# A LayerNorm's transposes moved from TensorE to a DMA in 16-bit halves, with rings of their own

## The chip, the core and the metric

The kernel runs on one core of one Trainium2 chip. The metric is device time in microseconds (us) of one launch, the median of several runs. A core has TensorE (PE in the profile, its weight loads PEld), VectorE (DVE), ScalarE (ACT), GpSimd (POOL) and SyncE (SP), which here issues the DMA transfers. Each engine takes its instructions in a fixed order and waits on semaphores for data, and for a buffer to come free.

## The reference

One transformer block over 2048 rows of 512, with modulation from a condition vector `c`:

```python
mod = (_silu(c) @ w_mod).reshape(c.shape[0], 6, 1, -1)
sa, ca, ga, sb, cb, gb = (mod[:, 0], ..., mod[:, 5])
h = _layernorm(x) * (1 + ca) + sa
x = x + ga * attention(h, k_cache, v_cache, wq, wo)   # 32 heads of 128, 8 kv heads, last 512 keys
h = _layernorm(x) * (1 + cb) + sb
x = x + gb * ((_gelu(h @ w_gate) * (h @ w_up)) @ w_down)   # inner width 1792
```

All inputs and the output are fp32. The text below is about the second LayerNorm, for the first 1024 of the 2048 rows, and about the tiles that hold the products of the feed-forward part.

## The kernel before

**Numbers.** Every matmul operand is an fp16 pair: a high half (the value rounded) and a low half (the rest), so a product is three matmuls (`mm3`, L86). To make a pair, ACT copies the fp32 tile to the high half and POOL or DVE subtracts it for the low half (`halves`, L154; `split_post`, L738; `parts`, L1295).

**Rows and stages.** The rows come in 16 tiles of 128, a query block is four tiles, a half of the attention is two query blocks. Attention runs as 128 units (half, pair of heads, query block, head) of four steps each; a step is one 128x512 score tile. For step t PE makes the scores `ps` (two PSUM banks in turn), DVE their maximum `nm` (L982), ACT the exponential `ee` (L991), ACT and DVE the two halves of the probabilities (`high` L1001, `low` L1006), and SP transposes both halves by one DMA, `pt<-p` (L1012). Two units later PE multiplies by the values (`po`, `pv_tasks` L926); its first product of a unit needs all four transposes of that unit. `pv_post` (L772) turns `po` into an `ot` pair: ACT writes the high half, DVE the low half a step later. When the four heads of a set have their `ot`, PE multiplies them with the output weights (`py`, `y_tasks` L940), one row tile per unit, 12 matmuls a tile, and DVE adds the result to the tile's `acc` (L952).

**Order of the work.** In the attention part every engine follows the program's order (`manual_schedule`, L1536). Work is put into named places: `at(("w", step), fn)` runs at the end of a step, `sched` (L608) puts a load some steps before its first use. The main loop (L1539 to L1584) goes through a step as scores, maximum, low half and transpose of an older tile, exponential, high half of an older tile, three queued PE groups, then loads, then "w" places. In the feed-forward part SP keeps the program's order, and a planner orders the other engines by simulated times.

**Rings.** `pool.tile(..., tag, bufs)` takes a slot of the ring `tag`, any free one; if none is free, the first instruction that writes the new tile waits until all readers of an older tile are done. Those that matter here:

- `ot`, 12 slots of 2 KB a partition (`NOT`, L43): the attention's `ot` pairs; `sbc` (L130), written at the start and read by `mod_col` (L135, L137) up to step 286; four early tiles; and in the feed-forward part all `at` pairs.
- `raw`, 5 slots: loads that are used once; the `stage` tiles of the weight preparation (`staged`, L1341); and the `hf` tile of the second LayerNorm (L504).
- `acc` in PSUM, 5 banks: most PE results, and the transposed LayerNorm tile `pln` (L498).
- `rw`, 2 slots: raw weights; `h`, 14 blocks of transposed activations; `gs`, one slot.

**The second LayerNorm, first 1024 rows.** When a tile of the first half has its last `py`, `attn_final` (L958) stores it and starts `ln_tile(2, ...)` (L476) on the `acc` tile in place. `now` is the step at which that happens; the eight tiles have it some three to five steps apart, from step 258 on. The steps are put at `now` plus 1, 5, 8, 9, 10, 12, 13 (L965): `stat` (DVE statistics, POOL power), `norm` (POOL, L239), `turn` (PE: four fp32 transposes of 128x128 into one `pln` bank, L500), `affine` twice (ACT, two 128x128 pieces each, PSUM to the fp32 tile `hf`, L508; the second also stores `hf` to DRAM as `hs`), `parts` twice (ACT high halves L520, POOL low halves L522, into the blocks). At `now` plus 12 the next rows are loaded into the `acc` ring. The blocks are used in the feed-forward part, from about step 480 on.

**Weights for the feed-forward part.** From step 286 on `prep_set` (L1349) loads gate and up weights into `rw`, measures them (`f_spread`, L297: POOL after PE and DVE), and POOL scales them, splits them into `stage` tiles and makes their combinations (L1356); SP stores each `stage` tile and loads the next weights when the `rw` slots are free. The first set has its POOL work at steps 290 to 296, the next set's loads come at steps 296 and 297.

**Feed-forward part.** For each pair n of column blocks the gated product has four parts. For ten of the fourteen passes (`turned(n)`, L293) the output product is made from three of them and four differences: `sums_of` (L1300) makes, on POOL, the differences t1, t3, t2, t4 and their pairs (`parts`), which PE reads in `yt_tasks` (L1696).

Of the kernel before, what the change touches and what calls it, by code (L numbers as in the profile page):

```python
# [10 lines left out]
F32 = mybir.dt.float32  # L11
# [28 lines left out]
GU = 2.0 ** -38  # L40
PRE = 2.0 ** -20
TINY = 1e-36
NOT = 12  # L43
LDGAP = 1
NRAW = 5
NRW = 2
# [18 lines left out]
def block_kernel(ctx: ExitStack, tc: tile.TileContext, x, kT, v, wq, wo, wg, wu, wd, cT, wc, wm, out):  # L65
# [410 lines left out]
    def ln_tile(gen, i, src):  # L476
        jsc, jsh = ln_cols("a" if gen < 2 else "f")
        qb, i = divmod(i % (2 * QT), QT)
        st = {}

        def load():
            if gen == 2:
                st["x"] = src()
            else:
                st["x"] = raw("xs")
                dma(st["x"], src())

        def stat():
            ln_stat(st["x"], st)
            ln_power(st)  # L490

        def norm():
            if gen == 2:
                return pool_ts(st["x"], st["x"], st["mv"][:, 0:1], st["rs"], ALU.subtract, ALU.mult)
            nc.vector.tensor_scalar(st["x"], st["x"], st["mv"][:, 0:1], st["rs"], op0=ALU.subtract, op1=ALU.mult)

        def turn():
            st["ps"] = bank("acc", "pln", NACC)  # L498
            for dt in range(KT):
                nc.tensor.transpose(st["ps"][:, dt * P:(dt + 1) * P], st["x"][:, dt * P:(dt + 1) * P], ident)  # L500

        def affine(dts):
            if 0 in dts:
                st["f"] = raw("hf") if gen == 2 else tmp("hf")  # L504
            f = st["f"]
            for dt in dts:
                sl = slice(dt * P, (dt + 1) * P)
                nc.scalar.activation(f[:, sl], st["ps"][:, sl], AF.Identity,  # L508
                                     scale=cols[:, jsc, dt:dt + 1], bias=cols[:, jsh, dt:dt + 1])
            if KT - 1 in dts:  # L510
                dma(spilled(gen, qb)[:, :, i * P:(i + 1) * P], f.rearrange("p (k q) -> p k q", k=KT))

        def parts(act):
            o = slice(i * P, (i + 1) * P)
            f = st["f"].rearrange("p (k q) -> p k q", k=KT)
            for h, name in enumerate(("b11", "b21") if qb == 0 else (None, "b22")):
                if name:
                    t, src = block(gen, name), f[:, 2 * h:2 * h + 2, :]
                    if act:
                        nc.scalar.activation(t[:, 0:2, o], src, AF.Copy)  # L520
                    else:
                        nc.gpsimd.tensor_tensor(t[:, 2:4, o], src, t[:, 0:2, o], op=ALU.subtract)  # L522

        more = [lambda: parts(True), lambda: parts(False)]
        return load, [stat, norm, turn, lambda: affine((0, 1)), lambda: affine((2, 3))] + more

    TURN = {}

# [429 lines left out]
    def attn_final(ti):  # L958
        y1[ti] = dram.tile([P, D], F32, name=f"y{ti}")
        dma(y1[ti], acc[ti])  # L960
        if ti < 2 * QT:
            nxt = ti + 2 * QT
            own, steps = ln_tile(2, ti, lambda: acc[ti])
            own()
            for d, fn in zip((1, 5, 8, 9, 10, 12, 13), steps):  # L965
                at(("w", now[0] + d), fn)
            at(now[0] + 12, lambda: load_acc(nxt, rows_of(x, nxt)))
        else:
            ln_last(ti - 2 * QT)
# [294 lines left out]
    def f_items(q, hold=None):  # L1264
# [28 lines left out]
                    sums_of()  # L1293

        def parts(key, g, eng):  # L1295
            t = A[n, key] = pair("ot", "at", NOT)
            nc.scalar.activation(t[:, 0, :], g, AF.Copy)  # L1297
            eng.tensor_tensor(t[:, 1, :], g, t[:, 0, :], op=ALU.subtract)

# [484 lines left out]
```

## Time and profile before

| What | Time |
|---|---|
| median of three runs | 1743.84 us |
| lowest and highest of them | 1743.32 and 1745.21 us |
| the profiled execution | 1743.57 us |
| its span, first to last instruction | 1741.8 us |
| PE busy in the span | 1714.7 us |
| first and last transpose of the eight tiles | 700.4 and 775.5 us |

Times within the trace count from the start of the span. In a row of groups stand line, engine, operation, output tile, input tiles, shapes and count, then busy time, mean duration in ns, and the idle time of the engine just before with what ended it. In a row about one tile the three numbers are shortest, median and longest duration in ns, then first and last start in us. A row of a timeline has start, duration, engine, line and tiles; in brackets the idle time before it and what ended that. PE's matmuls overlap by about 0.16 us, so what a PE group costs is read from start to start.

### The profile page before, as it was taken

To read this page: it belongs to the slowest core of one execution; us is meant where nothing else is said; L and a number is where in the kernel's file an instruction comes from. 1 tells how busy PE (TensorE), PEld (TensorE's weight loads), DVE (VectorE), ACT (ScalarE), POOL (GpSimd) and SP (SyncE) were. 2 spreads that over 40 slices of the span, in tenths; PEclk is the share of its full clock that TensorE was granted. 3 is DMA by queue.
4 is the path that set the end of the run, shared out by engine and by line. 5 is a ranking of instruction groups with operands and counts; after the bars stand their busy time and mean duration, and the time that the engine had idled before them with its cause. 6 is when DMAs were issued, how large, how long until landed. Compare 5 with 4: busy or idle time off the path is not lost.

```text
span 1741.8 us, 26188 instructions
## 1 busy us (share of the span) xinstructions
PE 1714.7 (98%) x8022; PEld 787.0 (45%) x8022; DVE 1417.6 (81%) x2454; ACT 1258.5 (72%) x2813; POOL 1045.9 (60%) x1266
## 2 busy tenths in 40 slices
PE   7999999999999999999999999999999999999998
PEld 5444444444444444444444444444444444444443
DVE  7898898888888899888888788888886678556674
ACT  6988788888878777898778778787784554643344
POOL 4889778776788884654675665754621558313422
PEclk9999999999999999999999999999999999999999
DMA  7999999999999999999999999899986663743235
GB/s 236 218 205 211 213 214 207 223 206 221 215 217 228 205 205 187 212 213 230 201 219 224 208 223 220 186 235 218 197 180 150 187 177 128 191 139 100 91 97 167
DMA packets 690636, 339.82 MB, mean 195 GB/s; under 512 B 578880, under 2 KB 601408, under 8 KB 690496
## 3 DMA queue, kind: packets, MB, share of 16 engines
q1 hardware_dynamic: 690208, 337.63, 85.5%
q8 instruction: 63, 1.03, 0.3%
q14 instruction: 77, 0.63, 0.1%
q10 hardware_dynamic: 288, 0.52, 0.1%
HBM read 135.66 MB, written 61.87 MB: 113 GB/s over the span
## 4 chain that ended last, share of the span: by engine, by line
PE 82%; ACT 5%; DVE 5%; DMA 3%; POOL 2%; issue 2%; SPq 0%; ACTq 0%; DVEq 0%; POOLq 0%
PE py L90 19%; PE ps L90 17%; PE po L90 17%; PE qa L90 8%; PE fa L90 6%; PE qc L90 4%; PE fc L90 3%; PE ya L90 2%; PE qb L90 2%; PE fb L90 2%; PE yc L90 1%; ACT ee L991 1%; DMA yv<-yu 1%; ACT p L1003 1%; DVE nm L982 1%
## 5 line engine op out<-in xcount | busy, mean ns | idle before, releaser
L991 ACT ACTIVATE ee<-ps,nm 128x512 f32<-128x512 f32 x512 | 350.1, 684 | 191.9 <-DVE nm L982 189.3
L1008 DVE SCALAR_TENSOR_TENSOR p<-ee,rr,p 128x512 f16<-128x512 f32 x512 | 460.0, 898 | 4.5 <-ACT p L1003 3.9
L982 DVE TENSOR_REDUCE nm<-ps 128x1 f32<-128x512 f32 x512 | 350.4, 684 | 106.1 <-PE ps L90 103.2
L90 PE MATMUL ps<-k,qt 128*128 128x512 f16 x1536 | 414.9, 379 | 5.6 <-ACT ee L991 4.4
L1003 ACT ACTIVATE p<-ee,rr 128x512 f16<-128x512 f32 x512 | 364.6, 712 | 19.0 <-DVE rr L999 10.0
L90 PE MATMUL po<-pt,v 128*128 128x512 f16 x1536 | 373.0, 379 | 2.7 <-DVE kmax L183 1.4
L90 PE MATMUL py<-wo,ot 128*128 128x512 f16 x1536 | 371.5, 379 | 0.1
L90 PEld LDWEIGHTS <-w 128*128 128x128 f16 x2184 | 213.3, 98 | 263.3 <-issue 4.7
L90 PEld LDWEIGHTS <-v 128*128 128x128 f16 x1536 | 149.9, 98 | 184.9 <-DMA pt<-p 2.3
L90 PEld LDWEIGHTS <-ot 128*128 128x128 f16 x1536 | 150.3, 98 | 181.7 <-DVE ot L740 0.5
L90 PEld LDWEIGHTS <-qt 128*128 128x128 f16 x1536 | 145.9, 98 | 176.9 <-issue 4.7
L1303 POOL TENSOR_TENSOR fg<-fg 128x512 f32<-128x512 f32 x40 | 51.8, 1295 | 135.6 <-DVE fg L1287 103.0
L740 DVE SCALAR_TENSOR_TENSOR ot<-po,ot 128x512 f16<-128x512 f32 x128 | 87.7, 685 | 39.1 <-ACT ot L739 38.6
L1297 ACT ACTIVATE at<-fg 128x512 f16<-128x512 f32 x86 | 53.4, 625 | 64.8 <-DVE fg L1287 44.5
L991 ACT ACTIVATION_READ_ACCUMULATOR ee<-ps,nm 128x1 f32 x512 | 99.9, 195 | 0.0
L952 DVE SCALAR_TENSOR_TENSOR acc<-py,ysc,acc 128x512 f32<-128x512 f32 x128 | 94.7, 740 | 6.2 <-PE py L90 6.2
L235 POOL TENSOR_TENSOR lw<-lw,half__86 128x1 f32<-128x1 f32 x37 | 23.4, 633 | 104.2 <-DVE lw L185 104.1
L90 PE MATMUL fa<-t,w 128*128 128x512 f16 x336 | 83.6, 379 | 1.9 <-ACT u L885 1.4
L90 PE MATMUL qa<-t,w 128*128 128x512 f16 x348 | 84.9, 379 | 0.0
L397 POOL TENSOR_TENSOR rs<-rs,nhalf 128x1 f32<-128x1 f32 x32 | 18.8, 586 | 103.6 <-DVE rs L391 100.7
L739 ACT ACTIVATE ot<-po 128x512 f16<-128x512 f32 x128 | 73.8, 577 | 5.0 <-PE po L90 5.0
L1657 DVE SCALAR_TENSOR_TENSOR yt<-ya,dyc,yt 128x512 f32<-128x512 f32 x68 | 50.1, 745 | 22.1 <-PE ya L90 21.7
(241 smaller groups left out, 2794.0 us busy)
## 6 DMA issues: line engine op xcount, KB each, us to landing
w<-kept SPq DMA_DIRECT2D x123, 256.0 KB, 3.3
wo<-kept SPq DMA_DIRECT2D x70, 256.0 KB, 3.4
kept<-stage SPq DMA_DIRECT2D x61, 256.0 KB, 3.3
raw<-in_wo SPq DMA_DIRECT2D x56, 256.0 KB, 3.2
kept<-w SPq DMA_DIRECT2D x39, 256.0 KB, 3.4
rw<-in_wq SPq DMA_DIRECT2D x38, 256.0 KB, 3.2
hs<-hf SPq DMA_DIRECT2D x32, 256.0 KB, 2.9
pt<-p SPq DMA_TRANSPOSE x512, 3.5
```

The costliest lines, as they stand in the source:

```text
L90: nc.tensor.matmul(ps, a, b, start=first and n == 0, stop=last and n == 2, skip_group_check=chain)
L235: nc.gpsimd.tensor_tensor(out, out, half_, op=ALU.pow)
L739: nc.scalar.activation(t[:, 0, :], src, AF.Copy, scale=scale)
L740: return lambda: nc.vector.scalar_tensor_tensor(t[:, 1, :], src, scale, t[:, 0, :], op0=ALU.mult, op1=ALU.subtract)
L952: nc.vector.scalar_tensor_tensor(acc[ti], st["p"], by, acc[ti], op0=ALU.mult, op1=ALU.add)
L982: nc.vector.tensor_reduce(nm, E[t]["ps"], axis=AX.X, op=ALU.max, negate=True)
L991: nc.scalar.activation(e, E[t]["ps"], AF.Exp, bias=E[t]["nm"], scale=1.0, accum_out=sm[:, t % 2:t % 2 + 1])
L1003: nc.scalar.activation(p16[:, 0, :], E[t]["e"], AF.Copy, scale=E[t]["r"])
L1008: nc.vector.scalar_tensor_tensor(p16[:, 1, :], E[t]["e"], E[t]["r"], p16[:, 0, :], op0=ALU.mult, op1=ALU.subtract)
L1297: nc.scalar.activation(t[:, 0, :], g, AF.Copy)
L1303: nc.gpsimd.tensor_tensor(g[o], g[a], g[b], op=ALU.subtract)
L1657: nc.vector.scalar_tensor_tensor(YT[key], ps, by, YT[key], op0=ALU.mult, op1=ALU.add)
```

## The change

The change touches three places.

1. `ln_tile` for the second LayerNorm's first rows (gen 2) no longer transposes on PE. ACT writes the high fp16 half of the normalised tile, POOL the low half, both into one pair of a new ring `lnh` of four slots. SP transposes the pair by one DMA, as for the probabilities, into a tile with a single slot: for even tiles a new tag `lnt`, for odd tiles the ring `gs`. POOL adds the two transposed halves into an fp32 tile `hf`, which also lies in `lnh`. ACT's affine then reads and writes that tile in place. `raw` holds no `hf` any more, and PSUM no `pln` of these tiles.
2. The steps are put at `now` plus 1, 5, 8, 9, 12, 16, 19, 20, 22, 23: statistics and `norm` as before, high half, low half, DMA transpose, sum, the two affines, the two block halves.
3. The ring `ot` has 10 slots instead of 12. In the feed-forward part the pairs of t1, t2 and t3 lie in `lnh`, that of t4 in `lnt`; the other `at` pairs stay in `ot`.

```diff
-NOT = 12
+NOT = 10
...
+        def high():
+            st["h"] = pair("lnh", "lnh", 4)
+            nc.scalar.activation(st["h"][:, 0, :], st["x"], AF.Copy)
+
+        def low():
+            nc.gpsimd.tensor_tensor(st["h"][:, 1, :], st["x"], st["h"][:, 0, :], op=ALU.subtract)
+
+        def turn_dma():
+            st["t"] = pool.tile([P, 2, KT, P], F16, tag="gs" if i % 2 else "lnt", name="lnt", bufs=1)
+            nc.sync.dma_start_transpose(st["t"].rearrange("p h k q -> p (h k) q"), st["h"].rearrange("p a b -> p (a b)"))
+
+        def joined():
+            st["f"] = pool.tile([P, D], F32, tag="lnh", name="hf", bufs=4)
+            nc.gpsimd.tensor_tensor(st["f"].rearrange("p (k q) -> p k q", k=KT), st["t"][:, 0], st["t"][:, 1], op=ALU.add)
+            st["ps"] = st["f"]
+
         def affine(dts):
-            if 0 in dts:
-                st["f"] = raw("hf") if gen == 2 else tmp("hf")
+            if 0 in dts and gen < 2:
+                st["f"] = tmp("hf")
...
-        return load, [stat, norm, turn, lambda: affine((0, 1)), lambda: affine((2, 3))] + more
+        turns = [high, low, turn_dma, joined] if gen == 2 else [turn]
+        return load, [stat, norm] + turns + [lambda: affine((0, 1)), lambda: affine((2, 3))] + more
...
-            for d, fn in zip((1, 5, 8, 9, 10, 12, 13), steps):
+            for d, fn in zip((1, 5, 8, 9, 12, 16, 19, 20, 22, 23), steps):
...
-            t = A[n, key] = pair("ot", "at", NOT)
+            t = A[n, key] = pair(*{"t4": ("lnt", "at", 1)}.get(key, ("lnh", "at", 4) if key[0] == "t" else ("ot", "at", NOT)))
```

## The prediction

> **What bounds the kernel now.** I read the profile page first, then the groups by engine, then busy time by stretch, then the timelines of PE, POOL, ACT and SP around the places that the diff touches.
>
> ```profile
> PE 1714.7 (98%) x8022; PEld 787.0 (45%) x8022; DVE 1417.6 (81%) x2454; ACT 1258.5 (72%) x2813; POOL 1045.9 (60%) x1266
> ...
> PE 82%; ACT 5%; DVE 5%; DMA 3%; POOL 2%; issue 2%; SPq 0%; ACTq 0%; DVEq 0%; POOLq 0%
> ```
>
> PE is the bound: 98% busy, and 82% of the chain. So a PE instruction that goes is time that goes, unless PE then waits for an engine that it used to be behind. The change lies where PE has little to give away but the others are loaded too:
>
> ```profile
> 700.00:800.00 100.00, 99.04 (x478) 47.01 (x477) 86.55 (x162) 85.78 (x212) 53.57 (x58) 1.00 0.99 213
> ```
>
> The columns are PE, PEld, DVE, ACT and POOL busy, the granted clock, and the DMA share, 0.99.
>
> **The change part by part.** *Out: the PE transposes.* Eight tiles with four transposes each are the 32 of this row:
>
> ```profile
> L508 ACT ACTIVATE hf<-pln,cols x64: 440/452/483, 239.3 to 782.0; 128x128 f32<-128x128 f32 x64
> ...
> L500 PE MATMUL pln<-ident,acc x32: 272/273/300, 700.4 to 775.5; 128*128 128x128 f32 x32
> ```
>
> Durations overlap on PE, so I price a tile by starts.
>
> ```profile
> 700.39 0.60 PE L500 MATMUL pln<-ident,acc 128*128 128x128 f32 x4
> 700.83 0.81 PE L90 MATMUL ps<-k,qt 128*128 128x512 f16 x3
> ...
> 730.84 0.81 PE L90 MATMUL po<-pt,v 128*128 128x512 f16 x3
> 732.28 0.63 PE L500 MATMUL pln<-ident,acc 128*128 128x128 f32 x4 [0.63 <-POOL w L158]
> ...
> 774.02 0.81 PE L90 MATMUL po<-pt,v 128*128 128x512 f16 x3
> 775.15 0.63 PE L500 MATMUL pln<-ident,acc 128*128 128x128 f32 x4 [0.33 <-ACT hf L508]
> ```
>
> From 700.39 to 700.83 a tile takes 0.44 us; eight are 3.5 us. A group of three matmuls takes about 0.65 us by starts (184.83 to 185.50, further down, is one), so the tile at 732.28 came 0.79 us late (1.44 less 0.65) and the one at 775.15 0.48 us late. Both waited for something only the transposes need (I read it as the PSUM bank that ACT still drains), so 1.27 us goes too. **Gross gain 4.8 us.**
>
> *In: split, DMA transpose, sum.* The nearest rows do the same operations elsewhere:
>
> ```profile
> L543 ACT ACTIVATE xh<-xs x8: 612/616/631, 1362.8 to 1399.3; 128x512 f16<-128x512 f32 x8
> L544 POOL TENSOR_TENSOR xh<-xs,xh x8: 1152/1161/1559, 1363.5 to 1401.3; 128x512 f16<-128x512 f32 x8
> L549 SPq DMA_TRANSPOSE xt<-xh x8: 1231/1240/1479, 1364.6 to 1410.4; - x8
> L522 POOL TENSOR_TENSOR b<-hf,b x24: 665/672/1124, 245.7 to 790.5; 128x256 f16<-128x256 f32 x24
> L1303 POOL TENSOR_TENSOR fg<-fg 128x512 f32<-128x512 f32 x40 | 51.8, 1295 | 135.6 <-DVE fg L1287 103.0
> ```
>
> Per tile: ACT 0.62 us, POOL 1.16 us for the low half, SP 1.24 us of issue. The sum of two f16 tiles into f32 is not in the trace: between 1.16 us (L544) and 1.30 us (L1303, all f32); I take 1.3, the row that also writes f32. ACT's affine now reads SBUF; I leave it at 0.45 us. ACT's 5 us over the eight tiles lie in its 14% of idle time. POOL's 2.5 us a tile are the problem. On SP the `pt<-p` transposes of the softmax stand in order behind each new issue, and on ACT each `ee` behind an affine that waits for the POOL sum.
>
> Against this stands a rule of the Trainium skill, VectorE: DVE Perf Modes, section "The three transpose paths": 390 ns on TensorE against 1309 ns by the DMA crossbar for one 128x128 of 16 bits, and TensorE is advised where PSUM will do. The trace is closer on issue (1.24 us for eight such blocks) and cheaper on PE (0.11 us a block); by that page's figures 32 blocks in two halves would trade an estimated 12.5 us of PE for 84 us of DMA, and the verdict would hang on who waits for the DMA.
>
> *Moved.* The affine and the block halves come ten steps later. Their readers are two hundred steps away, so this costs nothing by itself, but POOL's share of it lands later (below). The `raw` ring loses its `hf` tenants. In the new ring `lnh` a tile's first split on ACT can wait for a slot that POOL's block halves of an older tile free; I take 0, since any PE loss between 690 and 790 us that stays under 3 us is swallowed by the wait at 791 us below.
>
> *The ring of 12 becomes 10.* It isn't only for `ot`: `sbc` sits in it until its last reader.
>
> ```profile
> L137 DVE SCALAR_TENSOR_TENSOR wmc<-wmc,sbc x12: 674/684/1639, 643.3 to 755.0; 128x512 f32<-128x512 f32 x12
> ...
> 0.00:185.60 185.60, 23.63 (x96) 5.14 (x7) 1.00 0.93 217
> ...
> 0.00:182.50 182.50, 7.55 (x13) 1.00 0.93 216
> ```
>
> The two stretches count `py` alone and ACT's `ot` alone. Nine slots of ten are left to `ot` until 755 us. By 185.60 us PE has done 96 `py` matmuls (12 a row tile, so eight row tiles: the first set of four heads, both query blocks). ACT had written 13 `ot` tiles by 182.50. Four were done with (the first block's), nine were still held, the last four of the first set until that 96th matmul. The fourteenth finds no slot:
>
> ```profile
> 182.59 0.57 ACT L739 ACTIVATE ot<-po 128x512 f16<-128x512 f32 x1
> 183.06 0.62 ACT L218 ACTIVATE junk<-rw 128x512 f16<-128x512 f32 x1
> ...
> 183.68 0.67 ACT L991 ACTIVATE ee<-ps,nm 128x512 f32<-128x512 f32 x1
> 184.25 0.19 ACT L991 ACTIVATION_READ_ACCUMULATOR ee<-ps,nm 128x1 f32 x1
> ...
> 184.83 0.81 PE L90 MATMUL py<-wo,ot 128*128 128x512 f16 x3
> ...
> 185.50 0.81 PE L90 MATMUL ps<-k,qt 128*128 128x512 f16 x3
> ```
>
> ACT waits from 182.59 to about 185.55. Behind it stand `junk` and the exponential at 183.68, which must free the score bank for `ps` at 185.50. Its start comes 1.09 us after that of `ot` and its read ends 0.76 us later, now at 187.4: **PE loses 2.0 us** (bounds 0, if a slot comes free sooner, and 3.0). On DVE the low half of this `ot` stands in order before the next maximum and loses as much, but the next scores after 187.4 need it only at 190. In the later sets eight tiles are held when the next comes, and nine slots do.
>
> *The combinations.* In the feed-forward part t1 to t3 have four slots, t4 one. The tightest place:
>
> ```profile
> 1401.39 0.63 ACT L1297 ACTIVATE at<-fg 128x512 f16<-128x512 f32 x1 [0.41 <-POOL fg L1303]
> ...
> 1402.32 0.81 PE L90 MATMUL ya<-at,wo 128*128 128x512 f16 x3
> ```
>
> The first is t4 of the second pair, the other PE's last read of t4 of the first: ACT waits some 1.5 us, and PE reads the new t4 ten us later. I take 0 (bounds -1 and +1: the planner may order this part anew).
>
> *What is late next.* At 766 to 800 us the first feed-forward weights are prepared. This is the place that decides.
>
> ```profile
> 767.32 0.56 POOL L235 TENSOR_TENSOR lw<-lw,half__86 128x1 f32<-128x1 f32 x1 [6.42 <-DVE lw L185]
> ...
> 772.85 0.69 POOL L162 TENSOR_SCALAR rw<-rw,fsc 128x512 f32<-128x512 f32 x1 [0.98 <-DVE fsc L301]
> ...
> 787.60 0.62 POOL L158 TENSOR_SCALAR stage<-rw 128x512 f16<-128x512 f32 x1 [3.58 <-DMA kept<-stage]
> 788.30 1.16 POOL L159 TENSOR_TENSOR stage<-rw,stage 128x512 f16<-128x512 f32 x1
> ```
>
> ```profile
> pt<-p SPq DMA_TRANSPOSE x512, 3.5
> ```
>
> ```profile
> L96 SPq DMA_DIRECT2D hs<-hf x32: 319/534/917, 16.6 to 1422.0; - x32
> ```
>
> ```profile
> 789.48 0.35 SPq L96 DMA_DIRECT2D rw<-in_wu  x1
> ...
> 790.52 1.31 SPq L1012 DMA_TRANSPOSE pt<-p  x1
> ...
> 800.01 1.23 SPq L1012 DMA_TRANSPOSE pt<-p  x1
> ```
>
> ```profile
> 794.39 2.11 PE L90 MATMUL po<-pt,v 128*128 128x512 f16 x9
> ...
> 804.78 1.46 PE L90 MATMUL po<-pt,v 128*128 128x512 f16 x6
> ```
>
> POOL frees the second `rw` slot at 789.46; SP, in order, waits for it, and the transpose at 790.52, the fourth of its unit, stands behind. With the median flight of `pt<-p`, 3.5 us, it lands at 794.0, and `po` starts at 794.39: 0.4 us of slack. POOL's run from 767.32 to 789.46 is 22.1 us. Out of it go the 3.58 us wait (its slot was held by the `hf` tiles in `raw`), the 0.98 us wait and one block half, 0.67. Into it come the low halves of tiles 6 and 7 (2.3), the sums of tiles 4 and 5 (2.6) and the block halves of tiles 2 and 3 (four, 2.7). It is 24.5 us long. It starts when PE gets there: six tiles and one wait sooner (3.4), 2.0 later, so at 765.9, and ends at 790.4, 0.9 later than now. PE arrives at 791.6 (794.39 - 4.8 + 2.0) and waits until 794.9: **the gain is gone, and 0.5 us with it.** Then SP: its ten issues from 790.52 to 800.01 stand back to back; the transpose of tile 7 and the store of tile 5's `hf` come between (1.24, 0.53, and gaps: 1.9). The transpose of 800.01 goes out at 802.8 and lands at 806.3; PE wants it at 805.3: 1.0 us more.
>
> Sum: -4.8 + 2.0 + 3.3 + 1.0 = **+1.5 us**, on an execution of 1743.57 us (span 1741.8). Added to the median of the runs, 1743.84: **1745.4 us**.
>
> **The rivals.** *Gain kept (faster).* POOL's run at the weights ends by 786.9 instead of 790.4, because the sums or halves are done in POOL's idle time before, and the slot at 182.59 costs little. For it: POOL is idle 6.42 us just before 767.32. Against: the added pieces stand behind that spread in program order. Without either wait: -4.8, 1739.0; with the slot wait alone 1741.0.
>
> *POOL falls further behind (slower).* The same run, with pieces at the longer durations their rows show (L522 to 1.12, L544 to 1.56 us), adds about 3 us; each lands on PE one for one, as no slack is left: 1748.5. It counts as slower from 2 us on. For it: SP and ACT also wait for the late sums. Against: medians lie near the minima.
>
> *The clock.* The 3.3 us wait would be PE's longest since the start, and PE starts cold: the first transposes of the program take 417 to 455 ns, those of the rows above 272.
>
> ```profile
> 5.36 1.09 PE L129 MATMUL sps<-ident,silu 128*128 128x128 f32 x4 [5.36 <-DVE silu L126]
> ```
>
> ```profile
> L434 PE MATMUL pln<-ident,xn x16: 417/421/455, 14.0 to 17.4; 128*128 128x128 f32 x16
> ```
>
> From the first matmul at 5.36 to 17.4 that is 12 us at 272/421 of the speed, 4.2 us lost; the same again makes 1749.6. The Trainium skill, TensorE: Matmul & The Clock Gate, section "Why this matters for your kernels", says that gaps over about 3 us bring it back; the trace of before has no such gap mid-kernel and can't tell.
>
> **How the numbers follow.** Forecast 0.46, gain kept 0.20, POOL further behind 0.27, the clock 0.07. 0.2% is 3.5 us, about what a measurement of this kernel can tell from no change. The forecast's own range is 1742.5 to 1748; 0.06 of its chance lies over the line to slower, 0.01 over that to faster. Faster: 0.17 of the 0.20 (with the slot wait in full it is 1741.0 and inside the line) and that 0.01, 0.18. Slower: 0.24 of POOL's, 0.06 of the clock's and that 0.06, 0.36. Same: 0.46. The range goes from the gain nearly kept to the slower rival with the planner's +1 and a little: 1739.5 to 1750.0.
>
> **What would show it.** Right: no `pln` of `acc`; an ACT wait of 3 us before the fourteenth `ot` and a PE gap near 185.5; then PE waiting for `pt<-p` near 791 to 795, after POOL's second `rw` product ending near 790. Wrong: PE without a gap near either place; POOL through with `stage` before 787; or PE gaps at `ps` between 690 and 790, which would mean that ACT is the new bound.

## The result, and the profile after

| | before | changed |
|---|---|---|
| median of seven runs | 1744.6 us | 1750.6 us |
| lowest and highest | 1743.32 and 1745.49 us | 1747.62 and 1751.6 us |
| profiled execution, span | 1743.57, 1741.8 us | 1751.59, 1749.8 us |

The ratio is 1.0031, with a 95% interval of 1.0021 to 1.0041: **slower by 6 us**, just outside the range on record. Lines of the changed kernel are 17 higher than those of before from line 526 on (`ee` is L1008, `p` L1020 and L1025, `nm` L999).

The page of the changed kernel, busy time of each engine and the chain:

```profile
PE 1714.5 (98%) x7988; PEld 783.8 (45%) x7990; DVE 1420.8 (81%) x2454; ACT 1262.5 (72%) x2821; POOL 1067.7 (61%) x1282
...
PE 76%; DVE 8%; ACT 6%; DMA 4%; POOL 4%; issue 2%; SPq 0%; ACTq 0%; POOLq 0%; DVEq 0%
```

PE has lost the 32 transposes, yet 6 points of the chain have gone over to other engines. The same kernel, busy time by stretch (PE, PEld, DVE, ACT, POOL, clock, DMA):

```profile
700.00:800.00 100.00, 93.92 (x426) 41.78 (x425) 87.11 (x155) 84.25 (x201) 73.48 (x70) 0.98 1.01 213
```

POOL has 73.5 us of work here instead of 53.6, PE 93.9 instead of 99.0. To see where the time goes I set the starts of the scores `ps` of each step in the two traces side by side:

| step | before, us | changed minus before |
|---|---|---|
| 266 | 697.80 | -0.67 |
| 281 | 737.93 | -3.25 |
| 293 | 769.49 | -0.91 |
| 294 | 772.08 | +1.89 |
| 296 | 778.21 | +2.63 |
| 302 | 793.75 | +2.63 |
| 303 | 796.34 | +3.58 |
| 306 | 804.13 | +5.60 |
| 511 | 1319.32 | +5.65 |

The -0.67 comes from a wait at 546 us that is shorter in all later traces, those with the LayerNorm on PE too. So the change gains 2.58 us up to step 281, loses 2.3 again by 293, 3.5 by 296 and 3.0 from 302 to 306. Then nothing more happens until the feed-forward part.

What PE waited for from 700 to 830 us, first before, then in the changed kernel (total, times, longest):

```profile
PE pln L500 <- POOL w L158: 0.6, 1, 0.6
PE pln L500 <- ACT hf L508: 0.3, 1, 0.3
```

```profile
PE ps L90 <- ACT ee L1008: 5.4, 6, 2.6
PE qa L90 <- ACT u L902: 1.5, 2, 1.0
PE po L90 <- issue: 0.8, 1, 0.8
```

The two waits of the transposes are gone, and six waits for the exponential have come, and three others. Up to step 293 they are of two kinds. In some ACT is still busy with pieces of the LayerNorm when it should start `ee`, here an affine and a high half:

```profile
744.55 0.87 ACT L524 ACTIVATE hf<-hf,cols 128x128 f32<-128x128 f32 x2
745.32 0.62 ACT L504 ACTIVATE lnh<-acc 128x512 f16<-128x512 f32 x1
745.84 0.67 ACT L1008 ACTIVATE ee<-ps,nm 128x512 f32<-128x512 f32 x1
...
746.65 0.81 PE L90 MATMUL ps<-k,qt 128*128 128x512 f16 x3 [0.96 <-ACT ee L1008]
```

In others ACT itself sits idle for DVE's maximum. By the starts of `ps` the first kind delays PE by 1.6 us (at 746.65, 760.47 and 765.22), the second by 1.3 us (at 737.75, 751.92 and 768.57). The longest wait of all, on ACT, SP and PE, in the changed kernel's timelines:

```profile
769.28 0.58 ACT L756 ACTIVATE ot<-po 128x512 f16<-128x512 f32 x1
772.62 0.63 ACT L504 ACTIVATE lnh<-acc 128x512 f16<-128x512 f32 x1 [2.77 <-DMA lnt<-lnh]
773.16 0.67 ACT L1008 ACTIVATE ee<-ps,nm 128x512 f32<-128x512 f32 x1
...
768.59 1.40 SPq L511 DMA_TRANSPOSE lnt<-lnh  x1
...
769.22 2.10 PE L90 MATMUL py<-wo,ot 128*128 128x512 f16 x9
773.97 0.81 PE L90 MATMUL ps<-k,qt 128*128 128x512 f16 x3 [2.65 <-ACT ee L1008]
```

ACT wants to write the high half of the seventh tile. The slot of `lnh` that the tile was given is that of the sixth tile's pair, and it is free only when that pair's DMA transpose, issued at 768.59, has landed. Behind ACT's wait stands `ee`, behind that PE. And the granted clock falls to half for 3.41 us, which costs 1.7 (e1 below waits 2.3 us at the same place without the half clock, and stands 2 us better at step 296):

```profile
775.08:778.49 3.41, 3.41 (x10) 1.20 (x9) 3.06 (x8) 3.38 (x10) 2.55 (x4) 0.50 0.69 147
```

The place at the weights, on POOL, SP, PE and ACT of the changed kernel:

```profile
767.20 0.56 POOL L235 TENSOR_TENSOR lw<-lw,half__86 128x1 f32<-128x1 f32 x1 [7.09 <-DVE lw L185]
...
791.63 1.16 POOL L159 TENSOR_TENSOR stage<-rw,stage 128x512 f16<-128x512 f32 x1
...
784.86 1.23 SPq L1029 DMA_TRANSPOSE pt<-p  x1
789.42 0.34 SPq L96 DMA_DIRECT2D rw<-in_wu  x1
...
792.81 0.34 SPq L96 DMA_DIRECT2D rw<-in_wu  x1
793.21 0.55 SPq L96 DMA_DIRECT2D kept<-stage  x1
793.88 1.94 SPq L1029 DMA_TRANSPOSE pt<-p  x1
...
797.98 2.10 PE L90 MATMUL po<-pt,v 128*128 128x512 f16 x9 [0.79 <-issue]
...
803.76 0.72 ACT L1020 ACTIVATE p<-ee,rr 128x512 f16<-128x512 f32 x1 [3.46 <-DMA pt<-p]
```

POOL's run from the spread (767.20) to the second product (792.79) is 25.6 us long, 22.1 before. SP issues the `rw` load 0.02 us after it, then the fourth transpose of the unit, which lands at 797.89, and `po` starts at 797.98 instead of 794.39. Then SP is behind with its transposes, so that ACT waits 3.46 us for a slot of `p`, and PE twice more for ACT.

### The profile page after: what moved, and what is told of

It is laid out like the page before. It is cut to its first block, busy times and chain, and to the rows that moved or that the text cites. A ratio compares the mean times of both kernels' runs of the same rounds, so it can differ in the third digit from the quotient of the medians.

```text
span 1749.8 us, 26126 instructions
## 1 busy us (share of the span) xinstructions
PE 1714.5 (98%) x7988; PEld 783.8 (45%) x7990; DVE 1420.8 (81%) x2454; ACT 1262.5 (72%) x2821; POOL 1067.7 (61%) x1282
## 4 chain that ended last, share of the span: by engine, by line
PE 76%; DVE 8%; ACT 6%; DMA 4%; POOL 4%; issue 2%; SPq 0%; ACTq 0%; POOLq 0%; DVEq 0%
PE py L90 17%; PE po L90 16%; PE ps L90 16%; PE qa L90 7%; PE fa L90 6%; PE qc L90 4%; PE fc L90 2%; PE ya L90 2%; PE qb L90 2%; DVE p L1025 2%; DVE nm L999 2%; PE fb L90 1%; ACT ee L1008 1%; ACT p L1020 1%; PE yc L90 1%
## 5 line engine op out<-in xcount | busy, mean ns | idle before, releaser
L1008 ACT ACTIVATE ee<-ps,nm 128x512 f32<-128x512 f32 x512 | 349.7, 683 | 188.9 <-DVE nm L999 186.5
L1025 DVE SCALAR_TENSOR_TENSOR p<-ee,rr,p 128x512 f16<-128x512 f32 x512 | 462.1, 902 | 11.5 <-ACT p L1020 11.1
L999 DVE TENSOR_REDUCE nm<-ps 128x1 f32<-128x512 f32 x512 | 350.2, 684 | 96.2 <-PE ps L90 93.3
L1020 ACT ACTIVATE p<-ee,rr 128x512 f16<-128x512 f32 x512 | 364.4, 712 | 22.0 <-DVE rr L1016 9.8
L1008 ACT ACTIVATION_READ_ACCUMULATOR ee<-ps,nm 128x1 f32 x512 | 99.8, 195 | 0.0
L1674 DVE SCALAR_TENSOR_TENSOR yt<-ya,dyc,yt 128x512 f32<-128x512 f32 x68 | 50.3, 746 | 24.1 <-PE ya L90 23.7
```

The lines of the kernel that those rows point to most:

```text
L999: nc.vector.tensor_reduce(nm, E[t]["ps"], axis=AX.X, op=ALU.max, negate=True)
L1008: nc.scalar.activation(e, E[t]["ps"], AF.Exp, bias=E[t]["nm"], scale=1.0, accum_out=sm[:, t % 2:t % 2 + 1])
L1020: nc.scalar.activation(p16[:, 0, :], E[t]["e"], AF.Copy, scale=E[t]["r"])
L1025: nc.vector.scalar_tensor_tensor(p16[:, 1, :], E[t]["e"], E[t]["r"], p16[:, 0, :], op0=ALU.mult, op1=ALU.subtract)
L1674: nc.vector.scalar_tensor_tensor(YT[key], ps, by, YT[key], op0=ALU.mult, op1=ALU.add)
```

## The experiments

All in one table. The medians stand beside those of before on the same chip; the last three columns are starts of the scores against the first trace of before, as above. e16 leaves out half of the affine, so half of each tile's columns stay unscaled.

| kernel | median, us | before | ratio, 95% interval | step 266 | 296 | 307 |
|---|---|---|---|---|---|---|
| e1 LayerNorm alone | 1750.06 | 1744.36 | 1.0031 (1.0019 to 1.0042) | -0.46 | +0.68 | +5.12 |
| e2 rings alone | 1744.35 | 1744.36 | 1.0000 (0.9992 to 1.0009) | -0.60 | -0.62 | -0.54 |
| e3 DMA a step earlier | 1749.62 | 1744.36 | 1.0028 (1.0017 to 1.0039) | -0.35 | -1.64 | +5.25 |
| e4 four tiles of eight | 1747.18 | 1744.36 | 1.0017 (1.0008 to 1.0026) | -0.53 | +3.20 | +5.19 |
| e5 sum on DVE | 1751.31 | 1744.88 | 1.0033 (1.0021 to 1.0045) | -0.12 | +1.82 | +4.55 |
| e6 no sum, by halves | 1770.78 | 1744.88 | 1.0145 (1.0132 to 1.0158) | -0.36 | +15.02 | +23.72 |
| e7 POOL's queue | 1751.05 | 1744.88 | 1.0040 (1.0026 to 1.0054) | -0.51 | +0.64 | +5.98 |
| e8 before, POOL's queue | 1747.79 | 1744.88 | 1.0017 (1.0008 to 1.0026) | -0.34 | -0.38 | +3.84 |
| e9 weights 14 steps later | 1751.73 | 1744.67 | 1.0037 (1.0025 to 1.0050) | +0.01 | -1.29 | -0.83 |
| e10 before, the same | 1752.65 | 1744.67 | 1.0044 (1.0032 to 1.0056) | +0.77 | +0.23 | +0.23 |
| e11 e9, ACT spread | 1751.76 | 1744.67 | 1.0042 (1.0030 to 1.0054) | +0.10 | -1.63 | -1.49 |
| e12 before, POOL longer | 1748.42 | 1744.67 | 1.0019 (1.0010 to 1.0027) | -0.82 | -0.82 | +1.87 |
| e13 weights 25 steps apart | 1781.39 | 1745.07 | 1.0209 (1.0195 to 1.0223) | -0.66 | -1.97 | -1.17 |
| e14 before, the same | 1780.33 | 1745.07 | 1.0202 (1.0188 to 1.0216) | +1.00 | +0.46 | +0.46 |
| e15 e13, ACT spread | 1778.71 | 1745.07 | 1.0198 (1.0184 to 1.0212) | -0.53 | -2.63 | -2.63 |
| e16 e15, half the affine | 1778.96 | 1745.07 | 1.0194 (1.0180 to 1.0208) | -0.50 | -2.90 | -2.90 |
| e17 26 apart, ACT spread | 1763.61 | 1744.83 | 1.0105 (1.0089 to 1.0121) | +0.94 | -0.81 | -0.46 |
| e18 before, 26 apart | 1759.41 | 1744.83 | 1.0078 (1.0063 to 1.0092) | -0.76 | -1.31 | -1.31 |

My first theory was the slot: one long wait for `lnh` and the half clock behind it. The rival was load: POOL and ACT have too much to do, and that wait is only its face.

**Halves of the change (e1, e2).** In e1 the combinations go back to `ot`. e2 is the kernel before with `NOT = 10` and the line that e1 takes out.

```diff
-            t = A[n, key] = pair(*{"t4": ("lnt", "at", 1)}.get(key, ("lnh", "at", 4) if key[0] == "t" else ("ot", "at", NOT)))
+            t = A[n, key] = pair("ot", "at", NOT)
```

> The LayerNorm by DMA as in the changed kernel, ring ot of 10 slots; but the combinations t1 to t4 lie in ot again, as before. In the trace of the changed kernel the scores of step 320 start 5.6 us later than before, and the feed-forward part behind adds 2.4 us in the profiled run (8.0 us of span), 0.4 us in the medians (6.0 us). If the loss is all in the LayerNorm stretch from 700 to 810 us, this kernel is as slow as the changed one: 5.6 us over before, 1749.5 to 1751, and step 320 is 5.6 us late. If the rings of the combinations cost, it is 1 to 2 us faster than the changed kernel. If ten slots of ot are too few for all the pairs, it is slower than the changed kernel by 1 us or more.

> The other half of the change alone: LayerNorm on PE as before, ring ot of 10 slots, t1 to t3 in the ring lnh of four, t4 in lnt. If the loss is all in the LayerNorm stretch: the time of before within 0.7 us, 1744 to 1745.3, and PE without a gap near 185.5 us, since the changed kernel had none. If the feed-forward rings carry a part of the loss: 1 to 2.5 us over before, with PE idle between 1345 us and the end. The step of the prediction that put 2.0 us on the ring of ten at 185.5 us would give 1746.6 with that gap; the trace of the changed kernel already speaks against it.

The whole loss is the LayerNorm's; the rings cost nothing that the medians show (1.4 us less to 1.6 us more).

**The slot (e3) and half the tiles (e4).**

```diff
-            for d, fn in zip((1, 5, 8, 9, 12, 16, 19, 20, 22, 23), steps):
+            for d, fn in zip((1, 5, 8, 9, 11, 16, 19, 20, 22, 23), steps):
```

> The changed kernel with one number changed: the DMA transpose of a tile one step (2.6 us) earlier, at now plus 11. Theory of the slot: ACT's high half of the seventh tile waits 2.77 us for the slot of lnh that the pair before holds until its DMA has landed (772.54 us); PE idles 2.65 us behind it, and the granted clock falls to half for 3.41 us, which costs 1.7 us. One step earlier the DMA lands before ACT comes: the wait goes, the half clock with it, 4 us faster than the changed kernel: 1746 to 1747. Rival, load: ACT and POOL simply have too much work in this stretch, and PE's waits for the exponential only move; then under 1 us is gained: 1749.6 to 1751, with PE's waits at ps between 737 and 810 us about as long in sum (5.4 us in the changed kernel) but spread.

```diff
...
-        turns = [high, low, turn_dma, joined] if gen == 2 else [turn]
+        turns = [high, low, turn_dma, joined] if gen == 2 and qb == 0 else [turn]
...
```

> The first four tiles by DMA as in the changed kernel, the last four on PE as before, with their hf in raw; rings of the feed-forward part as in the changed kernel. By the starts of the scores the changed kernel was 3.25 us ahead of before at step 281 (0.7 of it from a wait at 546 us that has nothing to do with the change) and lost 8.9 us from step 282 to 306. If the loss begins only where the later tiles' ACT and POOL work meets the first feed-forward weights (767 us), this kernel keeps about 2 us: 1742 to 1743.5. If the pile-up of four tiles in a row is enough (ACT has the second affine of one tile and the high half of another in one step), it loses 1 to 2 us between steps 282 and 290: 1744 to 1746.

The theory of the slot fell. In e3 the wait at 772 us is gone and step 296 stands 4.3 us better than in the changed kernel; by step 307 nearly all of that is lost. What PE waited for in e3, 700 to 830 us:

```profile
PE ps L90 <- ACT ee L1008: 4.2, 5, 2.0
PE po L90 <- issue: 3.1, 1, 3.1
```

The 2.0 is a wait for a slot again, one tile later, and now for POOL's block halves:

```profile
779.98 0.63 ACT L504 ACTIVATE lnh<-acc 128x512 f16<-128x512 f32 x1 [1.66 <-POOL b L538]
...
781.33 0.81 PE L90 MATMUL ps<-k,qt 128*128 128x512 f16 x3 [2.01 <-ACT ee L1008]
```

So e3 is not a kernel without slot waits. What decides against the slot is the other wait, which the profile puts down to issue: it is the one for `pt<-p`, whose fourth transpose lands at 798.76, 0.09 us before `po` starts. It swallows what was gained ahead of it: at step 302 e3, e1, the changed kernel and e4 stand at +1.2, +1.8, +2.6 and +3.2, at step 307 all at 5.1 to 5.6. The starts in the traces, us:

| kernel | second `rw` load issued by SP | that unit's `po` on PE |
|---|---|---|
| before | 789.48 | 794.39 |
| changed | 792.81 | 797.98 |
| e1 | 792.93 | 797.97 |
| e3 | 792.35 | 798.85 |
| e4 | 794.02 | 798.71 |
| e5 | 792.98 | 798.49 |
| e12 | 791.43 | 796.26 |

So the new theory: POOL's run at the weights releases `rw`, that releases SP, and that PE, 4.7 to 6.5 us later. In e4, whose last four tiles are on PE, the run was 24.1 us long and began late, at 769.92, since PE, on whose result the spread waits, had lost 1.9 us near 760 us. Though only four tiles are left on the DMA there, e4 loses as much from step 281 to 296 as the changed kernel.

**Relieving POOL (e5, e6).** In e5 DVE does the sum. In e6 there is none: ACT's affine reads the high half, DVE adds the scaled low half, 128 columns at a time.

```diff
-            nc.gpsimd.tensor_tensor(st["f"].rearrange("p (k q) -> p k q", k=KT), st["t"][:, 0], st["t"][:, 1], op=ALU.add)
+            nc.vector.tensor_tensor(st["f"].rearrange("p (k q) -> p k q", k=KT), st["t"][:, 0], st["t"][:, 1], op=ALU.add)
```

> The changed kernel with one word changed: the sum of the two transposed halves on DVE instead of POOL. In the changed kernel, with the combinations in ot, with the transpose one step earlier and with four tiles only, the scores of step 307 start 5.1 to 5.6 us late, whatever was gained or lost before: PE waits near 796 us for pt<-p, which SP can issue only after the rw load, and that waits for POOL's run from the spread to the second product (22.1 us before, 25.6, 24.9 and 24.1 us). Theory of POOL's run: without two sums the run is 2.3 to 2.8 us shorter, and step 307 comes that much sooner: 2.5 to 3.3 us late, 1747 to 1748. Rival, general load: DVE (86 per cent busy) takes 0.7 us a tile more and delays the maximum as much as POOL was relieved: 1749.5 or more, with PE waits at ps.

```diff
+                if gen == 2:
+                    sc = cols[:, jsc, dt:dt + 1]
+                    nc.scalar.activation(f[:, sl], st["t"][:, 0, dt], AF.Identity, scale=sc, bias=cols[:, jsh, dt:dt + 1])
+                    nc.vector.scalar_tensor_tensor(f[:, sl], st["t"][:, 1, dt], sc, f[:, sl], op0=ALU.mult, op1=ALU.add)
...
-            for d, fn in zip((1, 5, 8, 9, 12, 16, 19, 20, 22, 23), steps):
+            for d, fn in zip((1, 5, 8, 9, 12, 17, 18, 21, 22), steps):
```

> No sum at all: ACT's affine reads the transposed high half, and DVE adds the low half times the scale to its result, 128 columns at a time (four small DVE instructions a tile). The affines stand at now plus 17 and 18, the block halves at 21 and 22, so that no affine falls in the step of a high half, and the seventh tile's pair gets another slot of lnh. POOL has 1.15 to 1.6 us a tile less, DVE an estimated 0.8 to 1.2 us more. Theory of POOL's run: as for the sum on DVE, step 307 at 2.5 to 3 us late, and the waits of 737 to 775 us mostly gone: 1746.5 to 1748. Rival, load of ACT and DVE: 1749 or more.

Both missed. In e5 the run is 24.3 us, 1.3 shorter, but begins 1.5 us later. What POOL saved was paid ahead of the run: at step 293 PE stands 2.1 us further back than in the changed kernel. e6 shows what it costs when two engines that each work in order hand small pieces back and forth; its waits from 720 to 840 us:

```profile
PE ps L90 <- ACT ee L1008: 20.9, 21, 2.8
DVE hf L522 <- ACT hf L521: 19.7, 14, 3.0
```

DVE waits for each small affine, and the maximum of the next scores behind it.

**Taking SP out of the chain (e7, e8).** POOL issues the six transfers itself.

```diff
-                dma(t, src)
+                (eng.dma_start if eng else dma)(t, src)
...
-        sched(b, (lambda: set_load(key, srcs, 0), [lambda: pair_stat(key, m, 0), nop]), b + 9, kind="rw")
+        sched(b, (lambda: set_load(key, srcs, 0, nc.gpsimd if q == 1 else None), [lambda: pair_stat(key, m, 0), nop]), b + 9, kind="rw")
```

> The changed kernel with the rw loads of the second gate/up set and the stage stores of the first one issued by POOL instead of SP: POOL stands behind its own products anyway, and SP's transposes of the softmax no longer do. Theory of POOL's run by way of SP: the wait for pt<-p near 796 us goes, and with it ACT's wait for a slot of p (3.46 us at 803.76) and PE's two gaps behind it; together 3.0 us from step 302 to 307. Step 307 is then 0.5 to 2.6 us late (what the slot wait and the half clock leave), 1746 to 1748. Rival: POOL and ACT are so far behind that the wait only changes its name; step 307 is 4.5 us late or more, 1749 or more. A POOL-issued transfer is not in any trace so far; if POOL takes over 1 us for each of the six, its own work comes later, but PE doesn't wait for it before the next set at about 812 us.

> The same six transfers moved to POOL, in the kernel before: the control. There po found its transposes 0.4 us ahead of time at 794.39 us, so PE doesn't wait for SP there. Theory of POOL's run: no difference, 0.3 us either way (1744 to 1744.7). If POOL's issues are dear, or the next set comes late, it is slower by 1 us or more; if SP's wait cost the kernel before something too, it is faster by as much.

The wait changed its name, as the rival said, and the control became slower. ACT of e8:

```profile
791.34 0.58 ACT L885 ACTIVATE u<-qa 128x512 f32<-128x512 f32 x1
797.06 0.63 ACT L218 ACTIVATE junk<-rw 128x512 f16<-128x512 f32 x1 [5.14 <-DMA rw<-in_wu]
```

POOL takes 0.56 to 0.78 us for each issue here and waits 5.10 us for one of its own stores to land, where it waited 3.58 us before, so `rw` is late. The late `rw` also holds ACT, whose sum of squares stands in order ahead of the exponential. So a late `rw` reaches PE by two ways.

**The direct test (e12) and the weights moved away (e9, e10, e11).**

```diff
             halves(outs[k][0]["t"] if k < 3 else outs[k][0]["t"][:, :, 0:256], src)
+            if q == 0 and k == 1:
+                for _ in range(2):
+                    tt(outs[k][0]["t"][:, 1, :], src, outs[k][0]["t"][:, 0, :], ALU.subtract)
```

> The kernel before, with POOL's subtraction for the third stage tile of the first set done three times over instead of once (the same values, 2 x 1.16 us): POOL's run is 2.3 us longer, as the changed kernel's was 3.5 us longer, and nothing else is changed. Theory of POOL's run: the second rw slot comes free at 791.8 instead of 789.46 us, po at 794.39 has 0.4 us of slack, so PE waits 1.9 us there, and SP's and ACT's backlog adds 1 to 2 us by step 307: 3 to 4 us late, 1747 to 1748.5. Rival: POOL's lateness there is covered (by the other rw slot, or by stages that nobody waits for): under 0.5 us at step 307, 1744 to 1745.3.

```diff
-        b = T // 2 + 30 + 27 * n
+        b = T // 2 + 44 + 27 * n
```

> The changed kernel with the preparation of the feed-forward weights 14 steps (36 us) later: b = T // 2 + 44 instead of 30. The run of POOL from the spread to the second product then starts at about step 304 and no longer holds the low halves, sums and block halves of six of the tiles. Theory of POOL's run: PE's wait for pt<-p near 796 us and what follows it (3.0 us from step 302 to 307) goes and nothing of the kind comes at the new place; what is left is the loss from steps 282 to 296, at most 2.6 us at step 300 with a half clock and about -1 without: 1743.5 to 1747. Rival, general load of POOL and ACT by the eight tiles: step 320 still 4.5 us late or more, 1749 to 1751.

> The same 14 steps later in the kernel before, as the control. PE did not wait at this place, so the theory of POOL's run gives the time of before within 0.7 us (1744 to 1745.5). If the later preparation itself costs or gains something further on (the last weights are ready 36 us later; less traffic beside the LayerNorm), this kernel shows how much, and the difference between the two later ones is what the LayerNorm by DMA is worth without the weights beside it.

e11 adds offsets chosen tile by tile:

```diff
-            for d, fn in zip((1, 5, 8, 9, 12, 16, 19, 20, 22, 23), steps):
+            for d, fn in zip((1, 5, 8, 9, 11, 15) + ((18, 19, 21, 22), (18, 19, 21, 22), (17, 18, 20, 21), (18, 19, 20, 21), (18, 19, 21, 22), (18, 19, 20, 21), (17, 18, 19, 20), (17, 18, 20, 21))[ti], steps):
```

> All that helped or may help: preparation 14 steps later, DMA transpose one step and sum one step earlier, and the affines and block halves of each tile in steps in which ACT has no high half and no other piece of a tile. Theory: with POOL's run out of the way, no slot wait and no two pieces on ACT in one step, the gross gain of 4.8 us is kept but for about 2: 1741 to 1743.5, faster than both kernels. Rival, load: ACT has 6 us more to do from 700 to 810 us (eight high halves of 0.62, 32 affines of 0.48 instead of 0.45) and its 14 per cent of idle time lies at the wrong places; then step 300 stays within 1 us of before and the time within 1743.5 to 1746.

e12 settles the place. POOL and PE in the kernel before with two subtractions more:

```profile
783.27 2.39 POOL L1356 TENSOR_TENSOR stage<-rw,stage 128x512 f16<-128x512 f32 x2
...
796.26 2.10 PE L90 MATMUL po<-pt,v 128*128 128x512 f16 x9 [2.52 <-DMA pt<-p]
```

2.39 us of POOL cost PE 2.7 us (from -0.82 to +1.87) and the medians 3.75, with no LayerNorm touched. The trace is that of the fastest of e12's eleven runs, so where the other 1 us went isn't shown. And e9 shows it the other way: with the weights later the +3.0 and the half clock are gone; PE's waits from 700 to 830 us:

```profile
PE ps L90 <- ACT ee L1008: 2.3, 6, 1.0
PE qa L90 <- ACT u L902: 0.5, 1, 0.5
```

e9 moves more than the weights, though: its seventh tile got another slot of `lnh`, so ACT's wait at 772 us is gone too, and e9 alone can't tell the two apart; e12 can. Step 307 then stands 0.84 us better than step 266, in the control 0.54. The total time doesn't show it: all three lose 7.5 to 9 us between steps 490 and 500, where the last weights now meet combinations. ACT of e9:

```profile
1291.11 0.63 ACT L374 ACTIVATE t<-cb 128x512 f16<-128x512 f32 x1 [5.41 <-POOL cb L591]
```

**What is left of the gain (e13 to e18).** Preparations closer together keep the last one near its place.

```diff
-        b = T // 2 + 30 + 27 * n
+        b = T // 2 + 42 + 25 * n
```

> The changed kernel with the weights' preparation 12 steps later at first and 25 instead of 27 steps apart, so that the last one is at its old place (the preparation 14 steps later throughout ran into the combinations near 1288 us and cost 8 to 9 us there, in the kernel before too). Theory of POOL's run: the scores of step 340 stand 0.8 to 1.1 us earlier against step 266 than in the kernel before, nothing is lost at 1288 us, and the time is within 1.5 us of before: 1743.5 to 1746. Rival: the loads of the sets, now two steps ahead of their use instead of three, hold ACT at each set; then both kernels with 25 steps are slower by 2 us or more.

> The control: the same order of the preparation in the kernel before. Theory: 1744 to 1745.5, step 340 at most 0.6 us earlier against step 266. Rival as for its pair: slower by 2 us or more, for the loads' sake.

> The 25 steps together with the spread pieces of ACT (DMA transpose a step earlier, affines and block halves where ACT has no other piece). With the preparation 14 steps later this order stood at -1.7 us at step 296 and -1.05 at step 340 against step 266. Theory: the same here, 1743 to 1745, the fastest of the kernels with the DMA, and no more than 1.5 us faster than before: ACT's load takes the rest of the gross 4.8 us. Rival: 1741 to 1742.5, if the waits at ps came from the place and not from the load.

```diff
-            for dt in dts:
+            for dt in () if gen == 2 and 0 not in dts else dts:
```

> As e15, but the second affine of each of the eight tiles leaves out its two ACT instructions (half of the columns stay unscaled; the store to hs stays). ACT then has 0.3 us a tile less than in the kernel before, instead of 0.7 us more. What is still open is where the gross gain of 4.8 us goes when POOL's run is out of the way. If it goes to ACT's load, PE's waits at ps between 740 and 790 us go and step 300 stands 4 to 4.8 us earlier against step 266 than in the kernel before: 1740 to 1741.5. If it goes to POOL's and DVE's sharing (DVE's low half of p takes 0.92 us in the mean in this stretch, 0.83 before), step 300 stays where it is in e15, within 0.7 us.

With `b = T // 2 + 40 + 26 * n`:

> The spread order of ACT's pieces with the preparation 10 steps later at first and 26 steps apart: the loads of a set are three steps ahead of their use as before (at 25 steps they were two ahead, ACT waited for rw up to 6.4 us at seven sets, and that cost 33 to 38 us), and the last preparation is 4 steps later than before. Theory: POOL's run doesn't hold PE, step 336 stands 2 us earlier against step 266 than in the kernel before, and nothing is lost later: 1742.5 to 1744.5, the version that could beat both. Rival: the last preparation, 4 steps later, already meets the combinations near 1288 us, as 14 steps later did: 3 us or more lost at step 500 in this kernel and in its control.

> The control: the kernel before with the same 26 steps. Theory: within 0.6 us of before at step 336 and at the end, 1744 to 1745.5, so that the difference to e17, some 1.5 us, is what the LayerNorm by DMA is worth where POOL's run doesn't bind. Rival: as there, 3 us or more lost at step 500.

In total time all six are misses, the controls too: each order of the preparation costs more further on than it gives here, at 25 steps because the loads come too late for ACT; what 26 steps cost, 14.6 us by step 490 in the control, was not followed up. ACT of e14, at the second pair of sets:

```profile
882.03 0.71 ACT L1003 ACTIVATE p<-ee,rr 128x512 f16<-128x512 f32 x1
888.62 0.63 ACT L218 ACTIVATE junk<-rw 128x512 f16<-128x512 f32 x1 [5.88 <-DMA rw<-in_wu]
```

In the stretch itself they do tell. From step 266 to 307 the LayerNorm by DMA gains 0.84, 0.51, 1.59, 2.10 and 1.40 us (e9, e13, e11, e15, e17), its controls 0.54 to 0.55, so over its control it is worth nothing to 1.6 us. The rest of the 4.8 us goes to the waits for `ee`. A part of them was ACT's own load: spreading its pieces, with the DMA transpose and the sum a step earlier, gained 0.75 us (e11 against e9) and 1.6 us (e15 against e13). What is left then is not: e16 takes another 0.96 us a tile off ACT and gains 0.3 in all, as the second branch of its expectation had it. In e15 and e16 ACT sat idle for DVE's maximum, 0.35 to 0.85 us, ahead of every `ee` that PE waited for (four in each), and DVE had no idle time before it. One of the four in e16, on DVE, POOL and ACT:

```profile
741.56 1.27 DVE L1025 SCALAR_TENSOR_TENSOR p<-ee,rr,p 128x512 f16<-128x512 f32 x1
742.75 0.68 DVE L780 TENSOR_TENSOR qb<-s,qb 128x512 f32<-128x512 f32 x1
743.35 1.19 DVE L137 SCALAR_TENSOR_TENSOR wmc<-wmc,sbc 128x512 f32<-128x512 f32 x1
744.47 0.68 DVE L999 TENSOR_REDUCE nm<-ps 128x1 f32<-128x512 f32 x1
...
742.25 1.75 POOL L538 TENSOR_TENSOR b<-hf,b 128x256 f16<-128x256 f32 x2
743.95 1.60 POOL L515 TENSOR_TENSOR hf<-lnt 128x512 f32<-128x512 f16 x1
...
745.18 0.69 ACT L1008 ACTIVATE ee<-ps,nm 128x512 f32<-128x512 f32 x1 [0.51 <-DVE nm L999]
```

Beside POOL's two-input instructions DVE's low half of `p` and `wmc` take 1.27 and 1.19 us instead of 0.74 and 0.68, so the maximum is late, and with it ACT and PE. That DVE's order and load hold these four is read from the trace; that POOL beside it is the reason is argued from such rows, not tested alone, and at two of the four DVE's rows just ahead are at most 0.9 us long.

## Why the prediction was wrong, step by step

Two steps failed. ACT's added 5 us were put at nothing, and they cost PE time at `ps` and made POOL's run start late. And the term for what is late next, +4.3, was too small: `po` came 3.1 us later than forecast and the backlog behind it cost 1.0 us more.

**Out: the PE transposes, -4.8.** Right as a price: by step 281 four tiles and the first wait had gone, 4 x 0.44 + 0.79 = 2.55 us forecast, 2.58 measured.

**The ring of 12 becomes 10, +2.0.** Wrong. ACT and PE of the changed kernel:

```profile
182.50 0.58 ACT L756 ACTIVATE ot<-po 128x512 f16<-128x512 f32 x1
...
171.87 1.46 PE L90 MATMUL py<-wo,ot 128*128 128x512 f16 x6
183.52 0.81 PE L90 MATMUL py<-wo,ot 128*128 128x512 f16 x3
184.82 0.81 PE L90 MATMUL py<-wo,ot 128*128 128x512 f16 x3
185.50 0.81 PE L90 MATMUL ps<-k,qt 128*128 128x512 f16 x3
```

No wait, and `ps` at 185.50 as before (the sum itself was 0.1 off: 187.4 less 185.50 is 1.9). I held all four tiles of a set to the set's last `py`. Each tile is free after its own last read: the last row tile reads its four `ot` three matmuls each, and the first two were done with by 173 us.

**In `lnh` 0.** Wrong as a wait: ACT waited 2.77 us for a slot, PE 2.65, and the half clock came on top. Wrong in the holder too: in the changed kernel the slot waited for a DMA transpose, and only in e3 for POOL's block halves. Right in its reason, that the wait for `pt<-p` swallows it: at step 307 e1, e3 and the changed kernel stand within 0.5 us of each other.

**ACT's 5 us in its idle time, at nothing.** This failed: 2.3 us were lost, net of the transposes' gain, at `ps` and once at `qa` between steps 281 and 293, before any long wait, a sign that the prediction had named. ACT's own pieces delayed `ps` by 1.6 us there, DVE's late maximum by 1.3. With ACT's pieces spread out (e15) ACT's share is gone, while DVE still makes PE late.

**What is late next, +4.3.** The place and the chain were right: POOL's run, the `rw` slot, SP, `pt<-p`, PE, then SP's backlog; e12 shows it, and e9 agrees. The term was mis-sized. The run was put at 24.5 us from 765.9 to 790.4; it was 25.6 us from 767.20 to 792.79. It began 1.3 us later than forecast, as DVE's part of the spread stood behind a reduction of `gate` that had waited 1.01 us for ACT:

```profile
766.29 0.69 DVE L191 TENSOR_REDUCE gam<-gate 128x1 f32<-128x512 f32 x1 [1.01 <-ACT gate L151]
766.90 0.21 DVE L185 TENSOR_SCALAR lw<-pst 128x1 f32<-128x1 f32 x1
```

It was 1.1 us longer, mostly because a wait for `fsc` that the forecast took out stayed (0.73 us), the second low half took 1.61 us instead of 1.16, the `norm` in it 2.52 instead of 2.08 and the block halves 0.3 more; the two sums in it, at 1.15 us each, were shorter than the 1.3 assumed. From its end to `po` went 5.2 us instead of 4.5. So `po` came at 797.98 instead of 794.9, and the backlog after it cost 2.0 instead of 1.0. Together with the 0.67 at 546 us that is the 4.8 us by which step 307 was missed. PE itself waited only 0.79 us at `po`, not the 3.3 forecast, as it had lost the rest by then; in e3, which had lost less, that wait is 3.05 us. That the loss of 2.0 us at 185 us, which didn't come, and the 2.3 us at 737 to 769 us, which weren't forecast, are of one size is luck. By mechanism the rival "POOL falls further behind" (1748.5) was the nearest: pieces at the long end of their rows, as it said. The clock's 1749.6 is nearer as a number, but by luck, as the next paragraph shows.

**The clock.** It came, given a chance of 0.07, twice in the profiled run, but not as priced: 3.41 us at half speed, 1.7 us lost each time, where I had put 4.2; the first, behind the slot wait, was swallowed at `po`, which starts at 797.97 in e1 too, without a half clock. The span of the seven runs, 4.0 us against 2.2 before, fits that: the fastest has a mean clock of 1.000, the others 0.997 to 0.999.

**The combinations, 0.** Right (e2). But the profiled run, 5.65 us late at step 511, ended 8.0 late. The largest pieces are a PE gap of 1.99 us before 1395.11, where ACT had waited for a load of `xs`, and the half clock after it. All twelve kernels with eight tiles on the DMA idle 1.6 to 2.7 us there, the eight others 0.3 to 0.9, though e1's feed-forward instructions stand in the same order as before's. Why stays open.

## What to carry to other kernels

Price a step by the engine that must wait for it, not by the engine that it relieves: 3.5 us of PE were paid with 20 us of POOL, and POOL stood at the head of a chain with at most 0.4 us of slack. Before moving work to an idle engine, look for its run that releases a buffer (here `rw`) and follow the queue behind that release; lengthening that run by a dummy of 2 us, as in e12, tells in one run whether it binds. And a slot is free after its own last reader, so list readers tile by tile.

## What the runs showed of the hardware

**Idle time and the clock.** In all twenty traces from 100 us on, PE gaps of 1.4 to 1.8 us, as the brackets of the timelines give them, never brought the half clock (16 gaps); 1.90 to 3.05 us did so in 17 of 28 (two of these stand under 1 us apart before one spell), 3.27 us and more always (19). The half clock then lasts 3.413 or 6.827 us. The Trainium skill, TensorE: Matmul & The Clock Gate, section "What's actually happening", gives a free-running window of 3413 ns. Both lengths agree with it, and it would explain why gaps of one length differ; no run here tests that. The Trainium skill, same page, "Why this matters for your kernels", advises against gaps over about 3 us. These traces show the half clock at shorter ones: 1.99 us was enough in the changed kernel, at 1395.11.

**DVE beside POOL.** In the changed kernel from 690 to 830 us, the low half of `p` takes 0.74 us in the mean where POOL is idle (12 rows, at most 0.75) and 1.01 where it overlaps POOL's two-input instructions (28 rows, up to 1.73); `nm`, which reads PSUM, takes 0.67 to 0.69 in either case. The Trainium skill, SBUF — State Buffer, section "Who interferes with whom", says that a DVE instruction with two SBUF inputs contends with a GpSimd instruction that reads SBUF, and that one with at most one doesn't, outside DVE's two-port modes; the trace agrees.
